# Loads of queries and keys four steps earlier, VectorE's side work dealt to other steps, sums copied at a step's end: an attention kernel with a routed expert layer

## The chip, the cores and the metric

The kernel runs on one core of a Trainium2 chip. The metric is the device time of one execution in microseconds (us). A core has TensorE (PE in the rows; PEld is its weight load), VectorE (DVE), ScalarE (ACT), GpSimd (POOL) and SyncE (SP), which here only issues DMAs. Each engine works through its own instructions in order and waits on semaphores for the others.

## What is computed

Attention over 4 batches of 8 heads, 768 tokens, head size 64, in which a query sees only the keys of its hash bucket; then a layer of 8 experts, where each of the 3072 tokens goes to one expert.

```python
q_bits = (q @ proj > 0); k_bits = (k @ proj > 0)          # 6 bits per token
mask   = bucket(q_bits)[:, None] == bucket(k_bits)[None, :]
attn   = softmax(where(mask, q @ k.T / 8, -1e9))
x      = attn @ v                                          # [3072 tokens, 512]
e      = argmax(x @ w_gate)                                # one expert a token
out    = softmax(x @ w_gate)[e] * sigmoid(x @ w_output_gate)[e] * (relu(x @ w1[e]) @ w2[e])
```

## The kernel before

Heads are taken in 16 pairs (index `g`). A pair takes 12 steps, so there are 192 steps; step `s` is 128 queries of one head against all 768 keys. In this text a step's phase is `s` modulo 12.

**One step.** TensorE makes the scores in PSUM (L534, tile `ps_s`, two buffers). VectorE reads them once, masks them and takes the row minimum (L538, "the score pass"); this frees the buffer. ScalarE takes the exponential (L546), VectorE prepares the reciprocal of the sums for two steps at a time (L553, L554) and GpSimd multiplies by it (L556). Four steps later (`LAG`) TensorE transposes the result (L567) and ScalarE copies it out of PSUM (L568). In every third step, at phases 1, 4, 7 and 10, TensorE also does twelve matmuls with the values (L578): "a run". Two runs finish the sums of one half of the queries, which VectorE copies out (L581): at phase 1 for the first half and at phase 7 for the second.

**Side work.** While a pair is worked on, the next one is prepared, in steps given by a table `at[step]` that `plan` fills (L386) and the main loop empties at the end of each step (L877). For pair `g`, with `s0` the first step of the pair before it: its queries and keys are loaded (`load`, L390, at `s0 - 5`), projected to bits by TensorE (`project`, L402, L408, at `s0`), compared by VectorE (`threshold`, L415), split into a rounded part by GpSimd (`split_hi`, L492) and a remainder by VectorE (`split_lo`, L500, two halves a head), and copied to where the score matmuls want them by eight DMAs a head (`spread`, L509 to L517). `rows` transposes the sums on VectorE (L590) and stores them to DRAM (L597). For each batch of four pairs there is the routing, thirteen pieces of work in the steps of the batch after: logits on TensorE (L612), tokens (L622, L624), and on VectorE `best`, `choose` (L648 to L655), `gates` (L659 to L667), `ranks` (L682 to L687), `cols` (L199 to L216), `hot` (L221). After the third batch the busiest expert is picked (`pick`, L753), and its first tokens and weights are prepared in the last pairs' steps (`early_...`).

The order of a step's instructions on TensorE, VectorE, ScalarE and GpSimd is that of the program. SyncE's queue is ordered by the compiler's scheduler when the program is built; a DMA that waits there holds up all behind it.

```python
plan(s0 - 5, lambda g=g: load(g))
...
for j in range(2):
    plan(s0 + 1 + 2 * j, lambda g=g, j=j: split_hi(g, j))
    for n in range(2):
        plan(s0 + 4 + 3 * j, lambda g=g, j=j, n=n: split_lo(g, j, n))
    plan(s0 + 4 + 3 * j, lambda g=g, j=j: spread(g, j))
```

After the last step come the expert layers, whose code is not touched.

Of the kernel before, what the change touches and what calls it, by code (L numbers as in the profile page):

```python
# [19 lines left out]
B, H, S, D = 4, 8, 768, 64  # L20
# [40 lines left out]
def lsh_attention_then_moe(  # L61
# [307 lines left out]
    with ExitStack() as actx:  # L369
# [8 lines left out]
        batches = [dict() for _ in range(B)]  # L378
        blocks = {}
        sums = {}  # L380
        at, products = {}, {}


        LAG = 2 * GROUP
# [1 line left out]
        def plan(step, *fns):  # L386
            at.setdefault(step, []).extend(fns)
# [182 lines left out]
        def weighted(hb, c):  # L570
            g, hf = hb // 2, hb % 2
            st = pairs[g]
            if c == 0:
                st["av"] = ps_a.tile([P, HS], F32, name="ps_a")
            if c == NT - 1 and hf == 0:
                st["ot"] = gp.tile([P, S], F32, name="ot", bufs=4)
            for j in (1, 0):
                nc.tensor.matmul(st["av"][j * D:(j + 1) * D], st["v"][:, j, c], blocks[hb][j][:, c],  # L578
                                 start=(c == 0), stop=(c == NT - 1))
            if c == NT - 1:  # L580
                nc.vector.tensor_copy(st["ot"][:, hf * HS:(hf + 1) * HS], st["av"])  # L581

        def rows(g, hf, whole=True):

# [123 lines left out]
        for g in range(NP):  # L708
            s0 = 12 * (g - 1)
            if g >= 2:  # L710
                plan(s0 - 5, lambda g=g: load(g))
            if g >= 1:
                s0 += g == 1
                plan(s0, lambda g=g: project(g))
                plan(s0 + 1, lambda g=g: threshold(g))
                plan(s0 + 10, lambda g=g: load_v(g))
                for j in range(2):
                    plan(s0 + 1 + 2 * j, lambda g=g, j=j: split_hi(g, j))
                    for n in range(2):
                        plan(s0 + 4 + 3 * j, lambda g=g, j=j, n=n: split_lo(g, j, n))  # L720
                    plan(s0 + 4 + 3 * j, lambda g=g, j=j: spread(g, j))
            for hf in range(2 if g + 1 < NP else 1):
                for c in range(NT):
                    products.setdefault(12 * g + 6 * hf + 6 + LAG + c // RUN * RUN, []).append(
                        lambda hb=2 * g + hf, c=c: weighted(hb, c))
                if g + 1 < NP:
                    plan(12 * g + 6 * hf + 16, lambda g=g, hf=hf: rows(g, hf))
        for i, fn in enumerate(more_constants()):
            plan(18 + 2 * i, fn)
        for b in range(B - 1):  # L730
            r = routing(b)
            ns = (8, 10, 9, 10, 10, 13, 20, 16, 16, 22, 25, 26, 26) if b == B - 2 else (8, 10, 9, 10, 10, 13, 25, 22, 22, 34, 37, 38, 38)
            for n, fn in zip(ns, (lambda r=r: r["logits"](0, H // 2), lambda r=r: r["tokens"](0, H // 2),
                                  lambda r=r: r["logits"](1, H // 2), lambda r=r: r["tokens"](1, H // 2),
                                  r["best"], r["choose"], r["gates"], r["prefix"], r["ranks"],
                                  r["cols"], r["hot"], r["table"], r["entries"])):
                plan(12 * (H // 2) * (b + 1) + n, fn)
# [7 lines left out]

        late = 12 * (H // 2) * (B - 1) + 19

        def load_expert(idi, i):  # L750
            expert.append(nc.values_load(idi[0:1, i:i + 1], engines=(mybir.EngineType.SP,), min_val=0, max_val=E - 1))
# [61 lines left out]
        def early_turn(a):  # L813
            if a == 0:
                early["x"] = new_x0()
            turn(early["xg"][a], early["x"], a * CH, True)
# [12 lines left out]
                nc.gpsimd.tensor_tensor(lo, raw[:, (part - 1) * F // 2:part * F // 2], f32(hi), ALU.subtract)  # L829

        plan(late, pick)
        plan(late + 9, early_gather)
        for a in range(EARLY):
            plan(late + 15 + 3 * a, lambda a=a: early_turn(a))
        for cc in range(NCC):
            plan(late + (1 + cc if cc < 2 else 5 + 6 * (cc - 1)), lambda cc=cc: early_load(cc))
            for k in range(3):
                plan(late + 6 + 6 * cc + 2 * k, lambda cc=cc, k=k: early_w1(cc, k))

        with tc.manual_schedule(engines=MANUAL):  # L840
            load(0)
# [18 lines left out]
            for s in range(0, NSTEP + LAG):  # L860
                if s < NSTEP:
                    live[s] = scores(s)
                    late_soft.append(s)
                if s == 0:
                    first_low()
                    signed()
                while summed:
                    normal(summed.pop(0))
                if s in products:
                    for fn in products[s]:  # L870
                        fn()
                    softs()
                if 0 <= s - LAG < NSTEP:
                    transposed(s - LAG, live.pop(s - LAG))
                if s < 6 + LAG or s + 1 in products or s >= NSTEP - 1:
                    softs()
                for fn in at.get(s, ()):  # L877
                    fn()

            hctx.close()  # L880
            ep = ctx.enter_context(tc.tile_pool(name="ep", bufs=1, side="right", reuse_waits="tile"))
# [12 lines left out]
                w2s += w2_piece(ep, 0, f, "hl")  # L894
            for c in range(NT):
                weighted(2 * NP - 1, c)
                if c == 0:
                    rows(NP - 1, 0, False)
                if c == 2:
                    r["add_pair"](0, lp)  # L900
# [232 lines left out]
```

## Time and profile before

| | |
|---|---|
| time, median of 3 runs | 811.57 us (806.96 to 812.52) |
| the profiled execution | 806.28 us, span 804.6 us |
| TensorE busy | 767.8 us, 95% of the span |
| VectorE, ScalarE, GpSimd busy | 496.0, 466.6, 381.9 us |
| mean granted TensorE clock | 0.987 |

The span runs from the first to the last instruction of the profiled execution. The steps end near 486 us; the rest are the experts. A matmul's end is modelled, so a busy TensorE may still be slower than it could be; the spacing of the runs shows that better than the busy time.

### The profile page before, as it was taken

What the parts mean: (1) busy time and instruction counts of PE and PEld (TensorE: products, weight loads), DVE (VectorE), ACT (ScalarE), POOL (GpSimd) and SP (SyncE); (2) the same over time, 40 slices, a digit from 0 to 9 for tenths busy, and PEclk for the clock granted to TensorE, in tenths of its full rate; (3) what the DMA queues carried; (4) which work ended last, traced back from release to release, by engine and by line L of the source; (5) the groups of instructions that cost most, each with busy time, mean ns of one, the idle gap of its engine ahead of it and who ended that gap; (6) DMA issues with size and microseconds to landing.
All of it is one profiled execution on the core that took longest, in us unless ns stands there. A gap on an engine that the chain in (4) does not pass through costs nothing. (4 is left out here: it accounts for less than half of the span.)

```text
span 804.6 us, 13670 instructions
## 1 busy us (share of the span) xinstructions
PE 767.8 (95%) x4674; PEld 603.7 (75%) x4674; DVE 496.0 (62%) x1034; ACT 466.6 (58%) x934; POOL 381.9 (47%) x426
## 2 busy tenths in 40 slices
PE   6999999999889999889989998999999999999997
PEld 4676766677556657666666666898899999999895
DVE  4776677778567768667688755444444445364640
ACT  4888787778567767677766872143243435253331
POOL 4555535445325425435437766272717373727301
PEclk7999999999899999999999999999999999999999
DMA  4554453554453463454455533365443544445521
GB/s 157 126 136 93 106 125 85 119 129 91 94 129 90 112 144 77 110 121 96 114 158 111 133 73 73 106 205 174 139 138 125 173 141 156 148 150 156 189 76 38
DMA packets 84797, 98.86 MB, mean 123 GB/s; under 512 B 57999, under 2 KB 59439, under 8 KB 84720
## 3 DMA queue, kind: packets, MB, share of 16 engines
q1 hardware_dynamic: 79376, 84.58, 40.4%
q0 software_dynamic: 5200, 13.31, 5.1%
q8 instruction: 39, 0.64, 0.4%
q14 instruction: 38, 0.31, 0.1%
q10 hardware_dynamic: 144, 0.02, 0.0%
HBM read 59.49 MB, written 13.11 MB: 90 GB/s over the span
## 5 line engine op out<-in xcount | busy, mean ns | idle before, releaser
L556 POOL TENSOR_SCALAR sc<-sc,rsum 128x768 f32<-128x768 f32 x192 | 178.4, 942 | 237.8 <-DVE rsum L554 188.8
L538 DVE TENSOR_SCALAR_CACHE_REDUCE sc<-ps_s 128x768 f32<-128x768 f32 x192 | 181.5, 954 | 75.2 <-PE ps_s L534 73.3
L568 ACT COPY pts<-ps_t 128x384 f32<-128x384 f32 x384 | 165.0, 482 | 85.0 <-PE ps_t L567 85.0
L546 ACT ACTIVATE sc<-sc,mn 128x768 f32<-128x768 f32 x192 | 178.5, 936 | 34.6 <-DVE sc L538 33.9
L567 PEld LDWEIGHTS ps_t<-ident,sc 128*128 128x128 f32 x1152 | 131.5, 140 | 48.1 <-issue 33.1
L567 PE MATMUL ps_t<-ident,sc 128*128 128x128 f32 x1152 | 161.1, 276 | 3.4 <-ACT pts L568 2.1
L578 PE MATMUL ps_a<-pts,vt 128*64 128x384 f32 x768 | 139.8, 500 | 0.0
L534 PE MATMUL ps_s<-xr,xl 128*128 128x384 f32 x384 | 116.5, 385 | 6.1 <-DVE sc L538 4.8
L534 PE MATMUL ps_s<-yr,yl 76*128 76x384 f32 x384 | 100.9, 343 | 1.8 <-POOL yr L443 1.7
L313 PE MATMUL ps_s<-xh,w1h 128*128 128x256 f32 (+7 forms) x288 | 96.9, 336 | 0.5 <-DVE hl L324 0.4
L324 DVE SCALAR_TENSOR_TENSOR hl<-ps_s,hh 128x256 fp32r<-128x256 f32 (+8 forms) x40 | 34.0, 850 | 102.6 <-ACT hh L323 102.6
L578 PEld LDWEIGHTS ps_a<-pts,vt 128*64 128x64 f32 x768 | 49.9, 137 | 62.4 <-issue 56.1
L313 PE MATMUL ps_s<-xlo,w1h 128*128 128x256 f32 (+7 forms) x288 | 95.3, 331 | 0.0
L313 PE MATMUL ps_s<-xh,w1l 128*128 128x256 f32 (+7 forms) x288 | 95.1, 330 | 0.0
L287 POOL DMA_INDIRECT xq<-x_dram,idx x75 | 81.8, 1091 | 21.6 <-issue 20.8
L330 POOL DMA_INDIRECT out_dram<-yo,sid x29 | 31.3, 1080 | 117.6 <-ACT yo L329 59.5
L323 ACT ACTIVATE hh<-ps_s 128x256 fp32r<-128x256 f32 (+8 forms) x40 | 29.1, 727 | 98.0 <-PE ps_s L313 98.0
L534 PEld LDWEIGHTS ps_s<-xr,xl 128*128 128x128 f32 x384 | 58.9, 193 | 27.6 <-DVE sc L538 18.8
L534 PEld LDWEIGHTS ps_s<-yr,yl 76*128 76x128 f32 x384 | 71.1, 192 | 2.7 <-POOL yr L443 2.4
L500 DVE SCALAR_TENSOR_TENSOR yl<-qk,pj,xl 128x384 fp32r<-128x384 f32 x60 | 57.6, 999 | 0.0
L313 PEld LDWEIGHTS ps_s<-xh,w1h 128*128 128x128 f32 x288 | 54.2, 188 | 2.5 <-DVE hl L324 0.8
L313 PEld LDWEIGHTS ps_s<-xlo,w1h 128*128 128x128 f32 x288 | 54.1, 188 | 1.3 <-DVE xlo L270 0.2
(204 smaller groups left out, 1033.0 us busy)
## 6 DMA issues: line engine op xcount, KB each, us to landing
w_raw<-in_w_dram SPq DMA_DIRECT2D x36, 512.0 KB
qk<-in_qkT_dram SPq DMA_DIRECT2D x32, 384.0 KB
xh<-in_w_dram SPq DMA_DIRECT2D x14, 512.0 KB
xlo<-in_w_dram SPq DMA_DIRECT2D x14, 512.0 KB
vt<-in_v_dram SPq DMA_DIRECT2D x16, 384.0 KB
xr<-xl SPq DMA_DIRECT2D x30, 192.0 KB
yr<-xl SPq DMA_DIRECT2D x30, 192.0 KB
xr<-yl SPq DMA_DIRECT2D x30, 192.0 KB
```

The costliest lines, as they stand in the source:

```text
L287: nc.gpsimd.indirect_dma_start(out=xq[:, k * P:(k + 1) * P], out_offset=None, in_=x_dram.rearrange("n (a f) -> (n a) f", a=NB32), in_offse ...
L313: nc.tensor.matmul(ps, l, r, start=first and k == 0, stop=last and k == len(pairs) - 1)
L324: return lambda: nc.vector.scalar_tensor_tensor(hl, ph, 0.0, f32(hh), ALU.max, ALU.subtract)
L330: nc.gpsimd.indirect_dma_start(out=out[:, :], out_offset=bass.IndirectOffsetOnAxis(ap=sid[0:n, r, a:a + 1], axis=0), in_=yo[0:n], in_offse ...
L500: nc.vector.scalar_tensor_tensor(st["yl"][j][:, cs], st["qk"][j][:, cs], sgn, f32(st["xl"][j][:, cs]), ALU.mult, ALU.subtract)
L534: nc.tensor.matmul(ss[:, n, 0:HS], l[0:k, qs], r[0:k, n * HS:(n + 1) * HS], start=first, stop=not first)
L538: nc.vector.tensor_scalar(sc, ss[:, :, 0:HS], MASKED, None, ALU.min, ALU.min, accum_out=mn)
L546: nc.scalar.activation(pr, pr, AF.Exp, bias=mn, scale=-1.0, accum_out=sums[s // GROUP][:, k:k + 1])
L556: nc.gpsimd.tensor_scalar(live[s0 + k], live[s0 + k], rs[:, k:k + 1], 0.0, ALU.mult, ALU.add)
L567: nc.tensor.transpose(tr[:, c], pr[:, (3 * h + c) * P:(3 * h + c + 1) * P], ident)
L568: nc.scalar.copy(pts[:, 3 * h:3 * h + 3, t * P:(t + 1) * P], tr)
L578: nc.tensor.matmul(st["av"][j * D:(j + 1) * D], st["v"][:, j, c], blocks[hb][j][:, c], start=(c == 0), stop=(c == NT - 1))
```

## The change

Four things are changed. Loads are planned at `s0 - 9` instead of `s0 - 5`. The splits, thresholds, both halves of `rows` and the pieces of the routing get other steps: nearly all of VectorE's side work now stands in steps with a run. The copy of the sums is no longer issued with the run's last matmul but put on a list, which is emptied when everything else of the step has been issued. The preparation of the first expert comes later (`late` and its offsets).

```diff
             if c == NT - 1:
-                nc.vector.tensor_copy(st["ot"][:, hf * HS:(hf + 1) * HS], st["av"])
+                summed_up.append(lambda: nc.vector.tensor_copy(st["ot"][:, hf * HS:(hf + 1) * HS], st["av"]))
...
-                plan(s0 - 5, lambda g=g: load(g))
+                plan(s0 - 9, lambda g=g: load(g))
             if g >= 1:
+                hi, lo, sent = ((-1, 2), (1, 4, 4, 7), (5, 8)) if g > 1 else ((2, 4), (4, 5, 6, 7), (5, 7))
                 s0 += g == 1
-                plan(s0, lambda g=g: project(g))
-                plan(s0 + 1, lambda g=g: threshold(g))
+                plan(s0 if g > 1 else 3, lambda g=g: project(g))
+                plan(s0 + 1 if g > 1 else 3, lambda g=g: threshold(g))
...
-                    plan(s0 + 1 + 2 * j, lambda g=g, j=j: split_hi(g, j))
+                    plan(s0 + hi[j], lambda g=g, j=j: split_hi(g, j))
...
-                        plan(s0 + 4 + 3 * j, lambda g=g, j=j, n=n: split_lo(g, j, n))
-                    plan(s0 + 4 + 3 * j, lambda g=g, j=j: spread(g, j))
+                        plan(s0 + lo[2 * j + n], lambda g=g, j=j, n=n: split_lo(g, j, n))
+                    plan(s0 + sent[j], lambda g=g, j=j: spread(g, j))
...
-                    plan(12 * g + 6 * hf + 16, lambda g=g, hf=hf: rows(g, hf))
+                    plan(12 * g + 22, lambda g=g, hf=hf: rows(g, hf))
...
-            ns = (8, 10, 9, 10, 10, 13, 20, 16, 16, 22, 25, 26, 26) if b == B - 2 else (8, 10, 9, 10, 10, 13, 25, 22, 22, 34, 37, 38, 38)
+            ns = 7, 8, 9, 10, 10, 16, 28, 19, 19, 31, 34, 35, 35
...
-        late = 12 * (H // 2) * (B - 1) + 19
+        late = 12 * (H // 2) * (B - 1) + 22
...
-        plan(late + 9, early_gather)
+        plan(late + 14, early_gather)
         for a in range(EARLY):
-            plan(late + 15 + 3 * a, lambda a=a: early_turn(a))
+            plan(late + 21 + 3 * a, lambda a=a: early_turn(a))
         for cc in range(NCC):
-            plan(late + (1 + cc if cc < 2 else 5 + 6 * (cc - 1)), lambda cc=cc: early_load(cc))
+            plan(late + (1 + cc if cc < 2 else 5 + 5 * (cc - 1)), lambda cc=cc: early_load(cc))
             for k in range(3):
-                plan(late + 6 + 6 * cc + 2 * k, lambda cc=cc, k=k: early_w1(cc, k))
+                plan(late + 6 + 5 * cc + (0, 1, 3)[k], lambda cc=cc, k=k: early_w1(cc, k))
...
                 for fn in at.get(s, ()):
                     fn()
+                while summed_up:
+                    summed_up.pop(0)()
```

`ns` are the steps of the routing's pieces, counted from the first step of the batch after, in the order logits, tokens, logits, tokens, best, choose, gates, prefix, ranks, cols, hot, table, entries.

SyncE's queue around the load of pair 8's queries and keys (`qk`), before the change. The rows ahead of the load are copies of pair 7's operands.

```order
L516 DMA yr<-bt 12x384
L512 DMA xl<-xl 64x768
L517 DMA yl<-bt 12x384
L516 DMA yr<-bt 12x384
L517 DMA yl<-bt 12x384
L395 DMA qk<-in_qkT_dram 128x768 x2
L597 DMA x_dram<-xb 32x24x32 x4
L400 DMA vt<-in_v_dram 128x768
```

The same load on SyncE now; the copies that follow it are those of pair 7.

```order
L517 DMA yl<-bt 12x384
L597 DMA x_dram<-xb 32x24x32 x4
L400 DMA vt<-in_v_dram 128x768
L395 DMA qk<-in_qkT_dram 128x768 x2
L509 DMA xr<-xl 64x768
L510 DMA yr<-xl 64x768
L511 DMA xr<-yl 64x768
L516 DMA yr<-bt 12x384
L512 DMA xl<-xl 64x768
```

The load has moved ahead of sixteen DMAs that copy the operands of the pair before.

VectorE in a pair without routing, before, from phase 1 to the score passes after phase 4 (L581 copies the sums, L415 is the threshold, L590 a transpose of the sums, L500 the two halves of a remainder, L538 the score pass).

```order
L581 COPY ot<-ps_a 128x384
L415 TENSOR_SCALAR bt<-ps_m,pj 128x384
L538 TENSOR_SCALAR sc,mn<-ps_s 128x768
L553 TENSOR_SCALAR rsum<-rsum 128x2
L554 RECIPROCAL rsum<-rsum 128x2
L538 TENSOR_SCALAR sc,mn<-ps_s 128x768 x2
L553 TENSOR_SCALAR rsum<-rsum 128x2
L554 RECIPROCAL rsum<-rsum 128x2
L590 STREAM_TRANSPOSE xb<-ot 128x384
L500 SCALAR_TENSOR_TENSOR yl<-qk,pj,xl 128x384 x2
L538 TENSOR_SCALAR sc,mn<-ps_s 128x768 x3
```

The same place on VectorE now.

```order
L415 TENSOR_SCALAR bt<-ps_m,pj 128x384
L500 SCALAR_TENSOR_TENSOR yl<-qk,pj,xl 128x384
L581 COPY ot<-ps_a 128x384
L538 TENSOR_SCALAR sc,mn<-ps_s 128x768
L553 TENSOR_SCALAR rsum<-rsum 128x2
L554 RECIPROCAL rsum<-rsum 128x2
L538 TENSOR_SCALAR sc,mn<-ps_s 128x768 x2
L553 TENSOR_SCALAR rsum<-rsum 128x2
L554 RECIPROCAL rsum<-rsum 128x2
L500 SCALAR_TENSOR_TENSOR yl<-qk,pj,xl 128x384 x2
L538 TENSOR_SCALAR sc,mn<-ps_s 128x768 x3
```

At phase 4 the transpose is gone; at phase 1 half a remainder has come, and the copy stands last.

VectorE where the routing's `cols` (L199 to L216) stands, before, at phase 10.

```order
L590 STREAM_TRANSPOSE xb<-ot 128x384
L199 TENSOR_TENSOR t_ge<-rank,chki 128x30
L202 TENSOR_TENSOR t_oa<-t_ge 128x24
L204 TENSOR_REDUCE t_na<-t_ge 128x6
L206 SCALAR_TENSOR_TENSOR t_pos<-t_na,rank 128x6
L212 TENSOR_TENSOR t_rhs<-oneh,t_oa 128x192
L216 TENSOR_TENSOR t_rhs<-t_rhs,toki 128x192
L216 TENSOR_TENSOR t_rhs<-t_rhs,gate 128x192
L538 TENSOR_SCALAR sc,mn<-ps_s 128x768 x3
```

The same work now, at phase 7.

```order
L500 SCALAR_TENSOR_TENSOR yl<-qk,pj,xl 128x384
L199 TENSOR_TENSOR t_ge<-rank,chki 128x30
L202 TENSOR_TENSOR t_oa<-t_ge 128x24
L204 TENSOR_REDUCE t_na<-t_ge 128x6
L206 SCALAR_TENSOR_TENSOR t_pos<-t_na,rank 128x6
L212 TENSOR_TENSOR t_rhs<-oneh,t_oa 128x192
L216 TENSOR_TENSOR t_rhs<-t_rhs,toki 128x192
L216 TENSOR_TENSOR t_rhs<-t_rhs,gate 128x192
L581 COPY ot<-ps_a 128x384
L538 TENSOR_SCALAR sc,mn<-ps_s 128x768
```

It has left the step that had one transpose and come to one that has half a remainder ahead of it and the copy of the sums behind it.

## Rows read from the trace of the kernel before

**Rows 1.** The page: TensorE's busy time, its share of the span and its instructions.

```profile
PE 767.8 (95%) x4674; PEld 603.7 (75%) x4674; DVE 496.0 (62%) x1034; ACT 466.6 (58%) x934; POOL 381.9 (47%) x426
```

**Rows 2.** TensorE's waits over the span: the waiting line, whom it waited for; us in total, times, the longest.

```profile
PE ps_m L408 <- DMA qk<-in_qkT_dram: 10.3, 10, 2.5
PE ps_s L534 <- DVE sc L538: 4.8, 10, 1.4
PE ps_m L408 <- POOL pjc L95: 3.9, 1, 3.9
```

**Rows 3.** The timeline of TensorE in a pair without routing, only the rows of the runs (L578): start, duration (us), then the operation. They are the runs of phases 10, 1, 4, 7 and 10.

```profile
57.98 2.16 PE L578 MATMUL ps_a<-pts,vt 128*64 128x384 f32 x12
65.27 2.16 PE L578 MATMUL ps_a<-pts,vt 128*64 128x384 f32 x12
71.58 2.16 PE L578 MATMUL ps_a<-pts,vt 128*64 128x384 f32 x12
78.28 2.16 PE L578 MATMUL ps_a<-pts,vt 128*64 128x384 f32 x12
84.58 2.16 PE L578 MATMUL ps_a<-pts,vt 128*64 128x384 f32 x12
```

**Rows 4.** The timeline of the same pair at phases 4 and 7: VectorE's side work, the score pass behind it, and TensorE's weight load that waits for it (in brackets: us idle before, and what ended it).

```profile
73.68 0.56 DVE L590 STREAM_TRANSPOSE xb<-ot 128x384 f32<-128x384 f32 x1
74.16 2.29 DVE L500 SCALAR_TENSOR_TENSOR yl<-qk,pj,xl 128x384 fp32r<-128x384 f32 x2
...
76.37 0.94 DVE L538 TENSOR_SCALAR_CACHE_REDUCE sc<-ps_s 128x768 f32<-128x768 f32 x1
...
77.38 0.30 PEld L534 LDWEIGHTS ps_s<-xr,xl 128*128 128x128 f32 x2 [0.35 <-DVE sc L538]
...
79.56 0.17 DVE L554 RECIPROCAL rsum<-rsum 128x2 f32<-128x2 f32 x1
...
80.49 0.56 DVE L581 COPY ot<-ps_a 128x384 f32<-128x384 f32 x1 [0.76 <-PE ps_a L578]
```

**Rows 5.** The timeline of TensorE, rows of the runs: those before and after late loads (195.40 to 239.91 the first three stretches, 351.72 to 361.85 the last), and at 330.83 and 338.72 a stretch with the routing's table matmuls but no load.

```profile
195.40 2.16 PE L578 MATMUL ps_a<-pts,vt 128*64 128x384 f32 x12
...
207.09 1.55 PE L578 MATMUL ps_a<-pts,vt 128*64 128x384 f32 x4
...
216.78 2.16 PE L578 MATMUL ps_a<-pts,vt 128*64 128x384 f32 x12
...
229.78 2.16 PE L578 MATMUL ps_a<-pts,vt 128*64 128x384 f32 x12
...
239.91 2.16 PE L578 MATMUL ps_a<-pts,vt 128*64 128x384 f32 x12
...
330.83 2.16 PE L578 MATMUL ps_a<-pts,vt 128*64 128x384 f32 x12
...
338.72 2.16 PE L578 MATMUL ps_a<-pts,vt 128*64 128x384 f32 x12
...
351.72 2.16 PE L578 MATMUL ps_a<-pts,vt 128*64 128x384 f32 x12
...
361.85 2.16 PE L578 MATMUL ps_a<-pts,vt 128*64 128x384 f32 x12
```

**Rows 6.** The timeline around the first late load: the run of phase 7, the last copy of pair 7's operands on SyncE's queue, the load of pair 8, and the projection that waits for it.

```profile
189.08 2.16 PE L578 MATMUL ps_a<-pts,vt 128*64 128x384 f32 x12
...
198.36 0.71 SPq L517 DMA_DIRECT2D yl<-bt  x1
...
199.12 0.98 SPq L395 DMA_DIRECT2D qk<-in_qkT_dram  x2
...
202.66 0.84 PE L408 MATMUL ps_m<-qk,pjc 128*32 128x384 f32 x4 [1.58 <-DMA qk<-in_qkT_dram]
```

**Rows 7.** Busy time by stretch: the stretch, its length, busy us (and instructions) of PE, PEld, DVE, ACT and POOL, the granted TensorE clock as a share of 2.4 GHz, DMA's share, GB/s. The first stretch is that of the first late load; the others run from the first VectorE operation of `choose`, `gates`, `ranks` and `cols` to the score pass behind it.

```profile
201.90:208.80 6.90, 5.55 (x18) 2.25 (x20) 1.88 (x6) 2.27 (x5) 0.07 (x1) 0.65 0.76 175
273.07:274.81 1.74, 1.74 (x15) 1.67 (x14) 1.60 (x7) 1.13 (x3) 1.07 (x2) 1.00 0.00 0
303.24:304.78 1.54, 1.54 (x13) 1.50 (x12) 1.47 (x10) 1.05 (x3) 1.09 (x2) 1.00 0.00 0
293.13:294.67 1.54, 1.54 (x12) 1.50 (x12) 1.43 (x6) 0.79 (x3) 1.00 (x2) 1.00 0.11 24
197.98:200.73 2.75, 2.75 (x23) 2.68 (x22) 2.65 (x9) 1.81 (x6) 1.59 (x2) 1.00 0.28 44
```

**Rows 8.** The timeline at the first projection of the program.

```profile
15.45 1.51 PE L408 MATMUL ps_m<-qk,pjc 128*32 128x384 f32 x8 [3.90 <-POOL pjc L95]
```

**Rows 9.** The timeline: a run, the score pass behind `choose`, the next run; then the runs on either side of the third batch's routing.

```profile
269.81 2.16 PE L578 MATMUL ps_a<-pts,vt 128*64 128x384 f32 x12
...
274.81 0.96 DVE L538 TENSOR_SCALAR_CACHE_REDUCE sc<-ps_s 128x768 f32<-128x768 f32 x1
...
276.72 2.16 PE L578 MATMUL ps_a<-pts,vt 128*64 128x384 f32 x12
...
391.81 2.16 PE L578 MATMUL ps_a<-pts,vt 128*64 128x384 f32 x12
...
445.18 2.16 PE L578 MATMUL ps_a<-pts,vt 128*64 128x384 f32 x12
```

**Rows 10.** The instructions that touch tile `qk`, the row of the remainders: count, shortest, median and longest duration in ns, first and last start in us.

```profile
L500 DVE SCALAR_TENSOR_TENSOR yl<-qk,pj,xl x60: 575/1148/1264, 23.7 to 442.1; 128x384 fp32r<-128x384 f32 x60
```

More of the change, by code (lines that the diff above doesn't have):

```diff
@@ L380, in lsh_attention_then_moe @@
         sums = {}
-        at, products = {}, {}
+        at, products, summed_up = {}, {}, []
         LAG = 2 * GROUP
@@ L896, in lsh_attention_then_moe @@
                 weighted(2 * NP - 1, c)
+                while summed_up:
+                    summed_up.pop(0)()
                 if c == 0:
```

## The prediction

> **What bounds the kernel now.** I read the page first. TensorE is busy 95% of the span [rows 1], so only its waits, and what its busy time hides, can be won. Next come its waits: the reader is to see that the largest is not for VectorE or GpSimd but for the loads of queries and keys, 10.3 us in ten pieces, that the score passes cost 4.8 us and one wait at the start 3.9 us [rows 2]. Last, the spacing of the runs on TensorE's timeline, which shows what busy time hides. In a pair without routing four runs are 7.29, 6.31, 6.70 and 6.30 us apart [rows 3]. The first holds the projection. The last two hold the same matmuls, so 6.70 holds a stall of 0.39 us. I take 6.31 as the length of a plain stretch, 7.29 as that of one with a projection, and call anything above it excess.
>
> The 0.39 us is VectorE's. At phase 4 it does a transpose (0.56) and two halves of a remainder (2.29), and its next score pass starts at 76.37, which is 4.79 us after the run's start at 71.58; the score matmuls after next then wait for the buffer [rows 3, 4]. With `choose` in the step the pass starts 5.00 us after the run (269.81 to 274.81), and the stretch takes 6.91, an excess of 0.60 [rows 9]. Both say the same: a pass that starts later than 4.40 us after a run costs what it is late. That limit is my measure for every step below.
>
> **The loads.** The first late one shows the cause: SyncE issues the load at 199.12, behind the last copy of the pair before (198.36), and the projection gets its data at 202.66 [rows 6]. The copies wait for remainders on VectorE; the load needs none of them. The excess of the stretches that hold late loads:
> - 195.40 to 207.09: 11.69 - 7.29 = 4.40, and the stretch behind it 9.69, against 7.89 for one with the same table matmuls (330.83 to 338.72): 1.80;
> - 229.78 to 239.91: 10.13 - 7.29 = 2.84, and 351.72 to 361.85 the same, 2.84 [rows 3, 5];
> - the two late loads between these, at 297 and 328 us, 2.47 and 3.60 by the same reckoning.
>
> Six stretches, 17.95 us, more than the 10.3 us of named waits, since two short pieces of a projection take longer than one whole and the clock falls once. After the change the load stands ahead of the sixteen copies, behind only the stores and the values of the pair before. It is then issued a whole pair's copies earlier, many us before its projection, against the 3.54 us that the row shows from issue to first use. I take the whole 17.95 us away (bounds: 10.3 if the stretches stay long for another reason, 17.95). What is late next at that place is only the projection itself, which stretches without a wait already hold.
>
> In the first of these stretches the granted clock is 0.65 on the mean from 201.90 to 208.80, so TensorE spent most of it at 1.2 instead of 2.4 GHz [rows 7]; that explains 4.40 + 1.80 against the 2.84 of the others, 3.36 us. The Trainium skill, TensorE: Matmul & The Clock Gate, section "What's actually happening", says that half speed is the idle state and that activity lifts it. By that rule the fall goes with the wait. Yet the longest wait for a load, 2.5 us [rows 2], was not the one with the fall, so the trace agrees only in part; were the fall to come back elsewhere, the sum would be 3.36 us worse.
>
> **The start.** The first projection waits 3.90 us for a constant from GpSimd [rows 8]; it is moved two steps back, so two more score tiles go ahead of it. Bounds 0 and 3.9; I take 2.5, since GpSimd, still busy with the first pair's operands, also holds the first transposes.
>
> **VectorE's side work.** No operation is added or removed; the sums are of places. Durations: half a remainder 1.15 (half of 2.29), copy of the sums 0.56, transpose 0.56 [rows 4]. At phase 7 side work can begin 1.45 us after the run (78.28 to the end of L554 at 79.73); the copy now waits there for the run's end, 0.76 us, and after the change it stands last, where the run is over [rows 3, 4].
> - Phase 4 without the transpose: 4.79 - 0.56 = 4.23, inside the limit. Eleven stretches gain 0.39: 4.3 us.
> - Phase 7, now half a remainder and the copy: 1.45 + 1.15 + 0.56 = 3.16. Phase 1 has the threshold besides, shorter than half a remainder: at most 4.31. Phase 10, two transposes. All inside: 0. The cover is the run's 2.16 us of matmuls and the transposes behind it; if it fails, see the third rival.
> - Routing, per batch: `choose` goes behind phase 4's remainders, 4.23 + 1.74 = 5.97, 1.57 late; `gates` too, 4.23 + 1.54 = 5.77, 1.37 late; `ranks` at phase 7, 1.45 + 1.15 + 1.54 + 0.56 = 4.70, 0.30 late; `cols` at phase 7, 1.45 + 1.15 + 2.75 + 0.56 = 5.91, 1.51 late [rows 7]. That is 4.75, and 14.25 for three batches. `hot` joins two transposes at phase 10 and stays inside.
> - Against it stands what the old places cost: `choose` 0.60 and `gates` 0.4 in two batches, 2.0 us, and the third batch, whose routing is squeezed together: seven stretches from 391.81 to 445.18 are 53.37 us [rows 9], and 7 x 6.31 with one projection (0.98), the table (1.58) and 0.2 of prefix matmuls would be 46.93: 6.44 us.
>
> So 4.3 + 2.0 + 6.4 = 12.7 us go and 14.25 come: 1.5 us worse. Dealing out the plain work helps, moving the routing onto loaded steps takes it back. Bounds: 14.25 nothing, or twice that.
>
> Half a remainder took 575 ns at the shortest and 1148 at the median [rows 10]. The Trainium skill, GPSIMD Engine Reference, section "Key points", says that GpSimd shares its SBUF interfaces with VectorE and contends with its instructions of two SBUF inputs, as these are. By that rule the dealt-out halves stay long, since GpSimd's normalization falls in the same steps, and the sum above holds; by the shortest row they could halve, which is the first rival.
>
> **Other edits.** GpSimd's split goes to steps without a run, where it has idle time (47% busy [rows 1]); the late preparations keep their amount, and end at the same step: 0, with 2 us either way.
>
> **The sum.** -17.95 - 2.5 + 1.5 = -18.95 against the profiled execution's 806.28 us (span 804.6): 787.3, and 788 with `ranks` a little later than its sum. The median of the runs shown is 811.57, 5.3 above the profiled one; the lowest, 806.96, is close to it. If the new kernel's runs lie as high above its profile, they show 793; the range holds that.
>
> **The rivals.**
> 1. VectorE's room suffices. If halves run unshared in the heavy steps, two are 1.15 instead of 2.29: `choose` is 0.43 late, `gates` 0.23, `cols` 0.94, `ranks` 0; 4.8 us instead of 14.25, and with the whole 3.9 at the start 777. For it: the shortest row; against it: the median is close to the long one.
> 2. The load stays late: the stores ahead of it on SyncE's queue wait for transposes that now both stand at phase 10. Then only the start and VectorE's part move: 806.28 - 2.5 + 1.5 = 805. Against it: the copies no longer stand ahead, and the first pairs' loads come without a wait now.
> 3. The copies at a step's end hold the score pass in plain pairs as well. If phases 1 and 7 lose 0.39 each, as phase 4 does now, in 13 pairs, that is 10 us: 798. For it: phase 1 reaches 4.31 by my bound; against it: phase 7 does more today and loses nothing (78.28 to 84.58 is 6.30 [rows 3]).
> 4. Slower: the operand copies become the wait. Today the last copy of a pair is issued 9.28 us after the run of phase 7 starts (189.08 to 198.36 [rows 6]), and the head that needs it is scored about two stretches, 13 us, after that start. TensorE that no longer waits for loads arrives sooner. It decides from about 1.25 us of lateness a pair, where 15 pairs eat 18.75 us; at 1.8 us the time is 788 + 27 = 815. Against it: the second remainder is ready earlier than now, as one half instead of two stands in phase 7.
>
> **How the numbers follow.** My forecast 0.55, its own range 783 to 794; first rival 0.25; third 0.12; second 0.04; fourth 0.04. A measurement of this kernel tells about 1%, 8 us, from no change, so the line is at 798 on the scale of the profiled execution. Forecast, first rival and half of the third lie below: 0.86. Half of the third and the second: 0.10. The fourth: 0.04. The range goes from 776, the first rival with a little over, to 801, which takes in the third and the higher level of the runs.
>
> **What would show it.** Right: TensorE's waits name no load of queries and keys; stretches with a projection are 7.29 us everywhere; the clock stays at 2.4 GHz from the start's rise on; phase 4 takes 6.31 us in plain pairs; the stretches with `choose`, `gates` and `cols` are over a us too long, with VectorE's score pass as the releaser. Wrong: a wait for L509 to L517's copies, or plain stretches above 6.31 at phases 1 and 7, or routing stretches without excess.

## The result, and the profile after

The changed kernel takes 785.19 us (median of 4 runs, 782.89 to 786.27) beside 810.38 us (4 runs, 806.96 to 812.52) of the kernel before: ratio 0.969, 95% interval 0.965 to 0.973. I had said 788, own range 783 to 794. The profiled execution took 784.33 us with a span of 782.6, so 22.0 us of span are gone, against 18.95 in my sum.

The page's busy line, answering to [rows 1]: TensorE is busy 11.6 us less, though it does the same matmuls; busy time had held stalls and slow clock.

```profile
PE 756.2 (97%) x4674; PEld 602.3 (77%) x4674; DVE 481.9 (62%) x1034; ACT 466.8 (60%) x934; POOL 392.3 (50%) x426
```

TensorE's waits, answering to [rows 2] (total us, times, longest): the waits for queries and keys and for the start's constant are gone, the one for VectorE's score pass has nearly doubled, and the one for GpSimd's normalization has grown from 0.4 to 1.8.

```profile
PE ps_s L534 <- DVE sc L538: 8.9, 11, 2.4
PE ps_m L672 <- DVE ohb L655: 2.2, 1, 2.2
PE ps_t L567 <- POOL sc L556: 1.8, 2, 1.6
PE ps_m L227 <- DVE t_ob L221: 1.1, 1, 1.1
```

The first run and the last one inside the loop over the steps, before. One more run follows behind the loop, 4.21 us later in every kernel; in this text "the last run" is the one inside it.

```profile
31.38 2.16 PE L578 MATMUL ps_a<-pts,vt 128*64 128x384 f32 x12
...
486.39 2.16 PE L578 MATMUL ps_a<-pts,vt 128*64 128x384 f32 x12
```

The timeline of the kernel after, in order of time (start, duration, operation, in brackets the idle time before it). A row of a run with fewer than twelve matmuls is cut off by the end of its view; only its start is read. First the first run; then a pair without routing, answering to [rows 3, 4]; a stretch with `choose` [rows 9]; the places of the late loads [rows 5, 6]; the ends of the third batch's part; last a wait in the expert part (L179 is a piece of the preparation of the expert's weights).

```profile
28.83 1.51 PE L578 MATMUL ps_a<-pts,vt 128*64 128x384 f32 x8 [0.42 <-ACT pts L568]
...
55.05 2.16 PE L578 MATMUL ps_a<-pts,vt 128*64 128x384 f32 x12
...
62.34 2.16 PE L578 MATMUL ps_a<-pts,vt 128*64 128x384 f32 x12
...
68.66 2.16 PE L578 MATMUL ps_a<-pts,vt 128*64 128x384 f32 x12
...
70.75 1.13 DVE L500 SCALAR_TENSOR_TENSOR yl<-qk,pj,xl 128x384 fp32r<-128x384 f32 x2
...
71.04 2.43 POOL L556 TENSOR_SCALAR sc<-sc,rsum 128x768 f32<-128x768 f32 x2 [0.52 <-DVE rsum L554]
...
72.36 0.96 DVE L538 TENSOR_SCALAR_CACHE_REDUCE sc<-ps_s 128x768 f32<-128x768 f32 x1 [0.48 <-PE ps_s L534]
...
74.97 2.16 PE L578 MATMUL ps_a<-pts,vt 128*64 128x384 f32 x12
...
81.28 2.16 PE L578 MATMUL ps_a<-pts,vt 128*64 128x384 f32 x12
...
150.07 2.16 PE L578 MATMUL ps_a<-pts,vt 128*64 128x384 f32 x12
...
152.45 2.43 POOL L556 TENSOR_SCALAR sc<-sc,rsum 128x768 f32<-128x768 f32 x2 [0.87 <-DVE rsum L554]
...
153.22 0.81 DVE L648 TENSOR_SCALAR eq<-df 128x48 f32<-128x48 f32 x1
...
155.55 0.95 DVE L538 TENSOR_SCALAR_CACHE_REDUCE sc<-ps_s 128x768 f32<-128x768 f32 x1
...
157.47 2.16 PE L578 MATMUL ps_a<-pts,vt 128*64 128x384 f32 x12
...
170.07 1.95 SPq L395 DMA_DIRECT2D qk<-in_qkT_dram  x2
...
198.54 0.85 PE L408 MATMUL ps_m<-qk,pjc 128*32 128x384 f32 x8
...
219.15 2.16 PE L578 MATMUL ps_a<-pts,vt 128*64 128x384 f32 x12
...
226.44 2.16 PE L578 MATMUL ps_a<-pts,vt 128*64 128x384 f32 x12
...
350.71 1.51 PE L578 MATMUL ps_a<-pts,vt 128*64 128x384 f32 x8
...
430.55 0.87 PE L567 MATMUL ps_t<-ident,sc 128*128 128x128 f32 x6 [1.62 <-POOL sc L556]
...
462.52 1.83 PE L578 MATMUL ps_a<-pts,vt 128*64 128x384 f32 x10
...
471.25 2.37 POOL L179 TENSOR_TENSOR w2l<-w_raw,w2h 128x1024 fp32r<-128x1024 f32 x1
471.26 2.41 DVE L648 TENSOR_SCALAR eq<-df 128x48 f32<-128x48 f32 x1
...
474.67 0.20 PE L672 MATMUL ps_m<-ohb,tri 128*128 128x48 bf16 x1 [2.17 <-DVE ohb L655]
```

Subtract neighbouring run starts. The plain pair is 7.29, 6.32, 6.31, 6.31: phase 4 no longer holds 0.39. The stretch that was 10.13 is 7.29 (219.15 to 226.44). The load is issued 28 us ahead of its projection (170.07, 198.54). With `choose` the stretch is 7.40. The last run, at 486.39 before, starts at 462.52, 23.87 us earlier; the span is only 22.0 shorter, so 1.9 us were lost behind it. The busy time by stretch, answering to [rows 7], shows where (the clock is the third figure from the right):

```profile
201.90:208.80 6.90, 6.90 (x48) 4.86 (x45) 5.29 (x14) 5.46 (x13) 4.71 (x5) 1.00 0.24 52
474.00:480.00 6.00, 4.89 (x32) 4.79 (x33) 5.17 (x30) 0.38 (x1) 0.00 (x0) 0.72 0.23 33
```

The half-speed piece at the first late load is gone, but the granted clock, 0.72 on the mean, now falls to 1.2 GHz for part of 474 to 480 us, behind the 2.17 us wait of L672. "The clock stays at 2.4 GHz from the start's rise on", one of my signs of being right, did not come true. The row of the remainders [rows 10] is now:

```profile
L500 DVE SCALAR_TENSOR_TENSOR yl<-qk,pj,xl x60: 597/605/1273, 21.4 to 409.8; 128x384 fp32r<-128x384 f32 x60
```

The median half has gone from 1148 to 605 ns.

### The profile page after: what moved, and what is told of

The parts are those of the page before. It is cut to its first block, busy times and chain, and to the rows that moved or that the text cites. A ratio compares the mean times of both kernels' runs of the same rounds, so it can differ in the third digit from the quotient of the medians.

```text
span 782.6 us, 13644 instructions
## 1 busy us (share of the span) xinstructions
PE 756.2 (97%) x4674; PEld 602.3 (77%) x4674; DVE 481.9 (62%) x1034; ACT 466.8 (60%) x934; POOL 392.3 (50%) x426
## 5 line engine op out<-in xcount | busy, mean ns | idle before, releaser
L556 POOL TENSOR_SCALAR sc<-sc,rsum 128x768 f32<-128x768 f32 x192 | 190.1, 1002 | 201.8 <-DVE rsum L554 159.8
L538 DVE TENSOR_SCALAR_CACHE_REDUCE sc<-ps_s 128x768 f32<-128x768 f32 x192 | 182.8, 956 | 80.5 <-PE ps_s L534 75.2
L578 PE MATMUL ps_a<-pts,vt 128*64 128x384 f32 x768 | 138.0, 495 | 0.4 <-ACT pts L568 0.4
L578 PEld LDWEIGHTS ps_a<-pts,vt 128*64 128x64 f32 x768 | 49.4, 136 | 61.7 <-issue 54.3
L313 PEld LDWEIGHTS ps_s<-xh,w1l 128*128 128x128 f32 x288 | 54.9, 191 | 1.1
```

The costliest lines, as they stand in the source:

```text
L313: nc.tensor.matmul(ps, l, r, start=first and k == 0, stop=last and k == len(pairs) - 1)
L538: nc.vector.tensor_scalar(sc, ss[:, :, 0:HS], MASKED, None, ALU.min, ALU.min, accum_out=mn)
L556: nc.gpsimd.tensor_scalar(live[s0 + k], live[s0 + k], rs[:, k:k + 1], 0.0, ALU.mult, ALU.add)
```

## The experiments

Twelve runs, four to a set, each set on one chip beside the kernel before. "First to last" is the time from the first run's start to the last one's (before 455.01, after 433.69), which leaves the start and the expert part out; "tail" is from the last run to the span's end (before 318.2, after 320.1).

| run | edited kernel | first run at | first to last | tail | span | ratio to before, 95% |
|---|---|---|---|---|---|---|
| e1 | before | 32.26 | 436.05 | 319.1 | 787.4 | 0.969 to 0.980 |
| e2 | after | 30.06 | 432.61 | 319.9 | 782.6 | 0.960 to 0.971 |
| e3 | after | 31.30 | 432.71 | 320.0 | 784.0 | 0.966 to 0.977 |
| e4 | after | 29.17 | 441.66 | 318.7 | 789.5 | 0.972 to 0.983 |
| e5 | after | 29.27 | 433.41 | 327.7 | 790.4 | 0.969 to 0.980 |
| e6 | after | 29.28 | 433.34 | 326.1 | 788.7 | 0.968 to 0.980 |
| e7 | after | 28.94 | 430.68 | 328.6 | 788.2 | 0.962 to 0.973 |
| e8 | after | 29.26 | 430.17 | 326.7 | 786.1 | 0.964 to 0.973 |
| e9 | after itself | 28.72 | 433.59 | 320.1 | 782.4 | 0.969 to 0.980 |
| e10 | before | 31.20 | 440.67 | 317.9 | 789.8 | 0.980 to 0.991 |
| e11 | after | 29.91 | 427.32 | 318.1 | 775.3 | 0.959 to 0.970 |
| e12 | after | 29.18 | 427.16 | 319.0 | 775.3 | 0.960 to 0.970 |

The four of the second set (e5 to e8) have a tail of 326 to 329 us; those are read by first to last and by single stretches only.

### e1 and e2: the load alone, and all but the load

```diff
 e1, in before:
-plan(s0 - 5, lambda g=g: load(g))
+plan(s0 - 9, lambda g=g: load(g))
...
 e2, in after:
-plan(s0 - 9, lambda g=g: load(g))
+plan(s0 - 5, lambda g=g: load(g))
```

> The kernel before with one edit, the load of queries and keys planned nine steps ahead instead of five. Theory: the late loads cost the whole excess of their stretches, 17.95 us, clock fall included, so the profiled span goes from 804.6 to about 787, all projection stretches are 7.29, the plain pairs keep 7.29, 6.31, 6.70, 6.30 and the start keeps its wait of 3.9. Rival A: only the named waits go, 10.3 us (span 794), because the stretches stay long for VectorE. Rival B: the load alone does not get ahead of the operand copies, since it was the dealt-out remainders that let them go earlier (span 800 or more, waits for qk stay in the list).

Measured, timeline of e1 around the first late place:

```profile
175.38 1.78 SPq L395 DMA_DIRECT2D qk<-in_qkT_dram  x2
...
196.28 2.16 PE L578 MATMUL ps_a<-pts,vt 128*64 128x384 f32 x12
...
199.81 0.71 SPq L517 DMA_DIRECT2D yl<-bt  x1
...
201.90 0.85 PE L408 MATMUL ps_m<-qk,pjc 128*32 128x384 f32 x8
...
203.57 1.83 PE L578 MATMUL ps_a<-pts,vt 128*64 128x384 f32 x10
...
211.45 0.87 PE L578 MATMUL ps_a<-pts,vt 128*64 128x384 f32 x4
```

The copies are as late as before (199.81), the load no longer stands behind them, and the six stretches become 7.29, 7.88, 7.30, 7.55, 7.29 and 7.29: 4.40 + 1.81 + 2.83 + 2.47 + 3.60 + 2.84 = 17.95 us, the prediction's term to the last digit. Another 0.9 goes in two stretches of the routing (6.93 to 6.31, 8.01 to 7.69), so that first to last is 19.0 shorter. The theory holds. Rival A with its 10.3 falls, and so does rival B: no wait for qk is left in the list.

> The kernel after with one edit undone, the load of queries and keys again five steps ahead. Theory: the loads are late as before and cost what they cost there, 10 to 18 us over the span of 782.6 of the kernel after (793 to 800); with the excesses of the six stretches back. Rival: the dealt-out remainders alone already make the copies, and with them the load behind them, early enough; then the span stays within 3 us of 782.6 and TensorE's waits name no qk.

Measured: the theory fell. The span is that of the kernel after, and no wait for qk is in the list. Timeline of e2:

```profile
186.58 0.99 SPq L395 DMA_DIRECT2D qk<-in_qkT_dram  x2
...
195.98 0.71 SPq L517 DMA_DIRECT2D yl<-bt  x1
...
199.70 0.85 PE L408 MATMUL ps_m<-qk,pjc 128*32 128x384 f32 x8
```

At five steps ahead the load is still issued 13 us before its projection, and ahead of the last copies. So a second edit of the change frees the load as well, and the first one brings nothing beside it.

### e10: which edit that is

The load of the next pair at s0 - 5 and the copies of this pair's second half at s0 + 7 were planned for one and the same step, 12g - 5, the copies first. The change sends these copies at s0 + 8.

```diff
 in before:
-plan(s0 + 4 + 3 * j, lambda g=g, j=j: spread(g, j))
+plan(s0 + 4 + 4 * j, lambda g=g, j=j: spread(g, j))
```

> The kernel before with one number changed, the copies of a pair's second half sent at step 8 instead of 7, one step behind the step of the load; VectorE's and TensorE's orders are those of the kernel before, SyncE's has the load ahead of those copies. Theory: the late load is a tie of two plans at one step, so this step alone takes away the waits for qk and the long stretches, like the load at nine steps did: 18 to 19 us less up to the last run (436 instead of 455 from the first run to the last), span 785 to 788 on a chip without the stall. Rival: the remainders on VectorE are what makes copies and load late, so with the old remainders the stretches stay at 9.5 to 11.7 or the copies, now a step later, become the wait.

Measured: 14.3 us less from first to last (440.67). The waits for qk are gone, so the tie was the cause. But that is 4.6 us less than e1 gained, because the rival is right in its second half; e10's waits of TensorE and its timeline show it:

```profile
PE ps_s L534 <- DMA xl<-xl: 2.3, 3, 1.8
PE ps_s L534 <- DMA yl<-bt: 1.5, 2, 1.4
```

```profile
314.09 0.48 SPq L512 DMA_DIRECT2D xl<-xl  x1
...
316.77 0.58 PE L534 MATMUL ps_s<-xr,xl 128*128 128x384 f32 x2 [1.79 <-DMA xl<-xl]
```

With the old, late remainders the copies have no step to give; the stretches at 308.51 and 338.80 are 9.41 and 8.95 instead of 7.29, and two others are 0.4 to 0.5 us longer than in e1. In the kernel after and in e2 the remainders are dealt out earlier and no such wait is left. My fourth rival was a real mechanism, then, in another mix of edits.

### e3: the start

```diff
 in after:
-... else ((2, 4), (4, 5, 6, 7), (5, 7))
+... else ((1, 3), (4, 4, 7, 7), (4, 7))
...
-plan(s0 if g > 1 else 3, lambda g=g: project(g))
-plan(s0 + 1 if g > 1 else 3, lambda g=g: threshold(g))
+plan(s0, lambda g=g: project(g))
+plan(s0 + 1, lambda g=g: threshold(g))
```

> The kernel after with the second pair's projection, threshold, splits and copies at their old steps. Theory: the first run starts 2.5 us later than in the kernel after (31.4 instead of 28.8), the wait for pjc is back at about 3.9 and the span is 785. Rival: the start's gain is given back before the first late place, so the span is 782.6 within 0.5 us although the first run starts later.

Measured: first run at 31.30, 2.5 us later, as in the theory, with the wait for the constant back at 4.3; span 784.0, 1.4 above, because the 1.1 us wait for `t_ob` (the fourth row of the waits after) does not occur in e3: the stretch that holds it, the table's, is 8.10, not 8.99. The edit need not be the cause of that: the wait is also missing in e2, e4 and e5 (7.94, 7.90 and 8.08), and it is there in e6, e9 and e12.

### e4: the transpose in phase 4

```diff
 in after:
-plan(12 * g + 22, lambda g=g, hf=hf: rows(g, hf))
+plan(12 * g + 6 * hf + 16, lambda g=g, hf=hf: rows(g, hf))
```

> The kernel after with the transposes of a pair's first half again six steps earlier, in phase 4. Theory: phase 4 holds a transpose and its halves start later, so they meet GpSimd's normalization again (mean of a half back from 1.13 to about 1.15 and over) and the score pass starts beyond 4.40 us after the run: plain phase-4 stretches are 6.70 again, 11 of them 4.3 us, and choose and gates 0.56 us later each in three batches, 3.4 us: span about 790. Rival: what made phase 4 short is the order of the two engines, the halves starting ahead of GpSimd, not the transpose; then plain pairs stay at 6.31 and only the routing stretches grow, span 786 at most.

Measured: span 789.5, first to last 8.0 longer. Eight plain phase-4 stretches are 6.68 to 6.70 again (3.1 us). The stretches of `choose` grow by 0.34 to 0.48 each, those of `gates` by 0.63, 0.64 and in the third batch 1.81; the rest is in the third batch too, behind a 2.9 us wait with a clock of 0.61 after it. The timeline of e4, phase 4 of the same pair:

```profile
69.37 2.16 PE L578 MATMUL ps_a<-pts,vt 128*64 128x384 f32 x12
...
71.47 0.56 DVE L590 STREAM_TRANSPOSE xb<-ot 128x384 f32<-128x384 f32 x1
...
71.76 2.08 POOL L556 TENSOR_SCALAR sc<-sc,rsum 128x768 f32<-128x768 f32 x2 [0.53 <-DVE rsum L554]
...
71.95 2.29 DVE L500 SCALAR_TENSOR_TENSOR yl<-qk,pj,xl 128x384 fp32r<-128x384 f32 x2
...
74.17 0.94 DVE L538 TENSOR_SCALAR_CACHE_REDUCE sc<-ps_s 128x768 f32<-128x768 f32 x1
...
76.07 2.16 PE L578 MATMUL ps_a<-pts,vt 128*64 128x384 f32 x12
```

Read it against 70.75 to 72.36 of the kernel after. There the halves start 0.29 us ahead of GpSimd and take 1.13, GpSimd 2.43; here they start 0.19 behind it and take 2.29, GpSimd 2.08. So both theory and rival are right in part: the transpose matters less by its own 0.56 us than by letting GpSimd start first, which costs 1.16. The rival's "plain pairs stay at 6.31" is wrong. (The 1.13 in the expectation is the time of two halves; one takes 0.6.)

### e5: the copy's place

```diff
 in after:
-summed_up.append(lambda: nc.vector.tensor_copy(st["ot"][:, hf * HS:(hf + 1) * HS], st["av"]))
+nc.vector.tensor_copy(st["ot"][:, hf * HS:(hf + 1) * HS], st["av"])
```

> The kernel after with one edit undone, the copy of the sums issued again right behind its run's last matmul instead of at the step's end. Theory: VectorE waits for the run's end before the copy and only then does its side work, 0.7 us later; plain stretches have room for that and stay at 6.31 (phase 7: 2.16 + 0.56 + 1.15 = 3.87, below 4.40), but ranks and cols, behind the copy in phase 7, grow by 0.6 to 0.7 each in three batches: about 4 us, span 786.5. Rival: the scheduler places the side work ahead of the waiting copy anyway, so the edit moves nothing: span within 0.5 us of 782.6.

Measured: plain stretches 6.30 to 6.32; with `cols` 7.10, 7.11 and 8.20 against 6.79, 6.79 and 7.76; with `ranks` unchanged. That is 1.1 us, a quarter of the theory's 4: the copy at the step's end helps only where much stands behind it. Nothing of it is left from first to last (433.41 beside 433.69): two stretches behind the third batch's routing are 0.91 and 0.29 shorter, the first for want of the wait for `t_ob`.

### e6 and e7: the routing's old steps

The edits of the next five runs are given in short.

```diff
 in after, e6: ns of batches 0 and 1    e7: ns of the third batch, and late, as before
+8, 10, 9, 10, 10, 13, 25, 22, 22, 34, 37, 38, 38        (e6)
+8, 10, 9, 10, 10, 13, 20, 16, 16, 22, 25, 26, 26        (e7)
```

> The kernel after with the routing of batches 0 and 1 at its old steps (choose and gates in phase 1, ranks and cols in phase 10). Theory: the excess only changes places. In phase 1 with threshold and half a remainder choose is 0.8 late and gates 0.6, cols in phase 10 behind two transposes 0 to 0.9, ranks 0, against 1.09, 0.84, 0.48 and 0.07 in the kernel after: the span stays within 1.5 us of 782.6. Rival: the new steps are worth what the batch gained over my sum, 2.3 us a batch, and the span goes to 787.

Measured: from 127.88 to 206.72, the stretches of one batch's routing, it takes 78.84 us against 79.11 of the kernel after, and 78.86 against 79.10 in the next. The theory holds: moving the routing of these batches brings nothing.

> The kernel after with the third batch's routing and the late preparations at their old steps. From the run that opens that stretch to the last run the kernel before took 94.58 us and the kernel after 95.47. Theory: the squeezed routing loses as much in its own stretches as the dealt-out one loses in the pieces that moved behind it, and the span stays within 1.5 us of 782.6. Rival, as the prediction had it: the old steps cost 6.4 us of excess and the new ones 4.75, so the span is 784.3 or more.

Measured: from the run at 350.83 to the last at 459.62 it takes 108.79 us, 3.0 less than the 111.81 of the kernel after (350.71 to 462.52). Neither theory holds: the new steps of the third batch are worse than the old ones.

### e8, e11 and e12: other steps

```diff
 in after, e8: all three batches 7, 8, 9, 10, 10, 19, 31, 22, 22, 34, 37, 38, 38; gather late + 17, turns late + 24
 e11: e8's for batches 0 and 1, e7's for the third
 e12: e8's for batches 0 and 1; third 7, 8, 9, 10, 10, 19, 26, 22, 22, 31, 34, 35, 35; pick late + 1, gather late + 16
```

> The kernel after with choose and gates in phase 7 instead of 4, ranks and cols in phase 10 instead of 7 where the projection gives 0.98 us of room, and the gather and turns of the last batch three steps later. Theory (a score pass that starts beyond 4.40 us after its run costs what it is late, and 0.98 more is free in phase 10): choose 1.45 + 0.75 + 0.54 + 1.74 = 4.48, 0.1 late; gates, ranks and cols 0; so 2.4 us a batch go, 4.8 in the first two, and 1 to 2 in the third: span 776 to 778. Rival: the excess comes from GpSimd holding VectorE whatever the phase; then choose and gates keep 0.8 to 1.1 and the span stays at 781 to 783.

Measured: from 127.85 to 347.33, where the first two batches are routed, it takes 219.48 us against 223.29, 3.8 less where 4.8 were expected. The timeline of e8 shows phase 4 without `choose` (150.49 to 156.80), phase 7 with `gates` (183.27 to 189.63, 6.36), and a wait in the third batch. `cols` in phase 10 keeps 0.48 in both batches: its pass starts 5.86 us after the run, and 4.40 + 0.98 = 5.38 are free. The third batch gains nothing instead of the 1 to 2 expected (112.10 us to the last run, beside 111.81): what `choose` and `gates` save there is lost again at phase 10, which has no projection, so that `cols` stands bare:

```profile
150.49 2.16 PE L578 MATMUL ps_a<-pts,vt 128*64 128x384 f32 x12
...
156.80 2.16 PE L578 MATMUL ps_a<-pts,vt 128*64 128x384 f32 x12
...
183.27 1.19 PE L578 MATMUL ps_a<-pts,vt 128*64 128x384 f32 x6
...
189.63 1.83 PE L578 MATMUL ps_a<-pts,vt 128*64 128x384 f32 x10
...
419.33 1.01 PE L534 MATMUL ps_s<-xr,xl 128*128 128x384 f32 x2 [3.13 <-DVE sc L538]
```

> The kernel after once more, beside the next three, since the four kernels of the second set all show a stretch of 8 to 9 us of stalls and half clock near 510 us in the expert part that none of the first set shows. Both theories expect its stretches up to the last run to repeat within 0.1 us each; its span is 782.6 if the chip is without that stall and about 789 if it has it.

Measured: 784.79 us (784.17 to 786.05), the stretches repeat within 0.1, and there is no stall: span 782.4. In e6 one of TensorE's waits in that place looks like this ("issue": the engine waits for nothing that the profile shows):

```profile
512.25 0.49 PE L313 MATMUL ps_m<-w2h,hh 128*128 128x512 f32 x1 [1.07 <-issue]
```

> The kernel after with the routing of batches 0 and 1 as in the seventh and tenth phases (e8) and the third batch and the late preparations at the old steps (e7). Theory: the two gains add, since they lie in different stretches: 3.8 us from the first two batches and 3.0 us from the third, 6.8 us less up to the last run and a span 5 to 7 us below the kernel after of the same set. Rival: part of it moves into the expert part as the gain of the third batch did; then under 3 us.

> As the run before, but with the third batch's choose in phase 7, ranks in phase 10, gates two steps behind the run of phase 1, cols in phase 7 as in the kernel after, the pick one step and the gather two steps later. Theory: choose and gates lose their 0.94 and 1.35 of excess, the gather no longer holds GpSimd (1.6): up to 3.5 us less in the third batch than in the kernel after and with the first two batches 7 us, about as the run before. Rival: what leaves these stretches comes back in the table's and the gather's, as in e8, and only the 3.8 us of the first two batches are left.

Measured: 776.91 us (775.10 to 778.37) and 776.98 us (776.87 to 778.73), beside 784.79 of the kernel after on the same chip: 1.0% less, and the runs do not overlap. In e11 first to last is 6.3 shorter than in e9 and the tail 2.0 shorter, because the wait of L672 is 0.18 there and the clock does not fall; the start is 1.2 later. In e12 they are 6.4 and 1.1 shorter, with a start 0.5 later; the wait of L672 stays (2.08), the clock does not fall. Both theories hold; these are the shortest of all.

## Why the prediction was right, and which term was not

The parts of the 22.0 us. The loads are measured by e1, whose only edit they are; plain phase 4 is eight stretches of 0.39; the routing is what is left up to the last run.

| term | predicted | measured |
|---|---|---|
| start | -2.5 | -2.55 |
| loads, six stretches | -17.95 | -17.95 |
| loads, elsewhere (two stretches of the routing) | 0 | -1.0 |
| plain phase 4 | -4.3 | -3.1 |
| routing and other VectorE side work | +5.8 | +0.7 |
| expert part | 0 | +1.87 |
| sum | -18.95 | -22.0 |

**The loads** were sized rightly but for 1.0 us, and e1 shows them alone. The step "the copies wait for remainders; the load needs none of them" is also right. What I did not see is that the change frees the load twice: by planning it nine steps ahead and by sending the second half's copies one step later (e2, e10). I credited the first edit with what either gives.

**The start** was right (e3).

**VectorE's side work** is the step that failed, in size, and the errors go both ways. Of the eleven phase-4 stretches that I credited, eight are plain in the kernel after; in the other three the routing now stands. I forecast 14.25 us of excess in the routing stretches: `choose` 1.57, `gates` 1.37, `ranks` 0.30, `cols` 1.51 per batch. In the first two batches they are 1.09 and 1.08, 0.84 and 0.85, 0.07 and 0.07 (after the 0.20 for the prefix matmuls), 0.48 and 0.48: 2.5 us each; in the third 0.94, 1.35, 0.06 and 1.45, so 8.8 in all. The limit itself, 4.40 us after the run, held: the pass behind `choose` starts 155.55 - 150.07 = 5.48 after the run, 1.08 late, and the stretch is 1.09 too long; behind `gates` 5.24 and 0.84; behind `cols` 4.87 and 0.48; in e4 behind `choose` 5.82 and 1.43. (Only `ranks` is a tenth off: 4.56, and 0.07.) What was wrong was what I put into the limit: two halves at 2.29 us. e4 shows that they are that long only where GpSimd has started first, and the removed transpose was what let it. The rule that I quoted from the Trainium skill (GPSIMD Engine Reference, section "Key points"), that the two contend, agrees with the traces (the two halves take 1.13 us or 2.29). As I quoted it, it leaves open which of the two pays, and by taking it that VectorE would, I kept the long number. The first rival had this right for the halves, but not for what stands behind them: L648 takes 0.81 here beside the stretched normalization, against 0.17 in e7's third batch, where one half and not two stands ahead of it. In the third batch of the kernel after L648 takes 0.17 as well, but the second half 1.26, so one or the other pays. So the excess of 1.09 lies between the forecast's 1.57 and the rival's 0.43.

What the old places cost I had too low. I put them at 1.0 us a batch for the first two batches, but the stretches of one batch take 79.07 us in e1 (132.38 to 211.45) and 79.11 in the kernel after: the old places cost as much as the new ones.

The other error hides the first. I let 6.44 us go in the third batch. The seven stretches there did shrink, from 53.37 [rows 9] to 49.23 (367.05 to 416.28). The six behind them grew from 41.21 to 46.24: the table matmuls, the gather and the normalization that waits behind it (430.55, 1.62) moved there. Net +0.9, so the excess was displaced, and with the old steps it would have been 3.0 less (e7).

**The expert part** is 1.87 us longer, and about 1 of it is the clock, which fell in another place, a risk that I had put at 3.36. With the fall the tail is 319.1 to 320.1 (the kernel after, e1, e2, e3, e9), without it 317.9 to 319.0 (before, e4, e10, e11, e12). The nearest pairs are e9 and e12, 320.1 and 319.0 with a like wait of L672, and e1 and the kernel before, 319.1 and 318.2 with the same code there. What makes up the rest was not tried.

**The rivals**: the second (load stays late) and the third (copies at the end hurt phases 1 and 7) do not occur: qk has left the list and these stretches are 6.31. The fourth does not occur here and does in e10. That the sum is near is in part luck: the side work came out 3.9 us and the loads 1.0 better than forecast, the expert part 1.9 worse.

## What to carry to other kernels

Where a transfer is late, ask first what stands ahead of it on its queue and whether two plans fall on one step: one step's change of the copies took away every wait for the loads, as the four steps of head start did; alone it was worth 14.3 us against 19.0 (e10, e1), and with the earlier remainders as much (e2). Measure the limit of a resource on the timeline (here 4.40 us from the run to the next score pass): with it the excess of a stretch comes out to some hundredths of a us, and it also tells where side work is free, which gave the 1% of e11 and e12. Do not carry the duration of an operation into a place where its neighbour on another engine starts in another order, and follow dealt-out work to the end of the part it is dealt into.

## What had not been expected of the hardware

Of VectorE's two halves and GpSimd's two normalizations, the engine that starts second is stretched: 1.13 and 2.43 us one way, 2.29 and 2.08 the other. A normalization that meets no half takes 0.91 in both kernels, and the median of the 28 halves at phase 4 is 1.15 before and 0.6 after. The wait of L672 comes of the same: L648 takes 2.41 us where it starts 0.01 us behind GpSimd's L179 (471.25), and 0.19 in e11, where no L179 runs at that time and the wait is 0.18.

The granted clock does not follow the length of the wait alone, and what else decides stays open. Behind the wait of L672 it fell to 1.2 GHz in the kernel after (2.17 us of wait), e9 (2.24), e1 (1.88), e2 (2.08), e3 (2.22) and e7 (1.91), not in the kernel before (2.15), e4 (2.00), e5 (2.08), e6 (1.75), e8 (1.89), e10 (1.83) and e12 (2.08). The fall at the first late load is gone in every kernel whose load is early.

The stall near 510 us in all four of the second set and in none of the other ten profiles (up to 4.8 us of waits marked "issue", with the clock at half behind them) hardly comes from the edits: that of e6 ends over 150 us ahead of it, and the kernel before was slow beside that set too, 815.73 us against 808.66 and 807.43 beside the other two. The kernel after itself was not run beside it. The cause was not tried.
